# Weight-gradient blocks of a window-attention backward pass over six quads instead of three, one per step in one pair of PSUM banks

## The chip, the cores and the metric

The kernel runs on one core of a Trainium2 chip. The metric is the device time in microseconds (us) of the whole kernel; lower is better. Eight runs of the kernel before have a median of 2055.7 us (2049.22 to 2061.59).

## The reference

A picture of 256 × 256 points with C = 384 channels is cut into 1024 windows of 8 × 8 = 64 points. Each window does single-head attention with one projection for q, k, v and an output projection. The result is the output and, for a given gradient of it, the gradients of x, wqkv and wo.

```python
qkv = xw @ wqkv                                   # xw: 1024 windows x 64 points x 384
q, k, v = (qkv[..., :C].copy(), qkv[..., C:2 * C].copy(), qkv[..., 2 * C:].copy())
p = _softmax(jnp.einsum('bqc,bkc->bqk', q, k) * scale, axis=-1)
o = jnp.einsum('bqk,bkc->bqc', p, v) @ wo
...
_out, _vjp = jax.vjp(_f, x, wqkv, wo)
_grads = _vjp(grad_out)
```

All tensors are bf16.

## The kernel before, in words

**Tiles.** A "quad" is a block of 16 × 32 points, that is 8 windows, held as 4 tiles of 128 rows (two windows each) by 384 channels. There are 128 quads, and the main loop is `step(n)` for n = 0 to 127. Weights are folded once at the start: A = scaled Wq·Wkᵀ (with its transpose AT) and B = Wv·Wo (with BT), so that scores need one projection of x, and the gradient of the scores one projection of the output gradient DO.

**What a step does.** Step n works on three quads at once. For quad n it makes MD (`md`, L188: x and the turned probabilities TT), the two parts V and W that the weight gradients need together with most of dx (`attn`, L220, from P in PB), the rest of dx (`dxs`, L253) and the output (`outs`, L201). For quad n+2 it makes the scores and the softmax (`scores`, `chain0`, `chain2`, `chain3`, L127 to L161). For quad n+3 it projects x and DO (`proj`, L109) into YHT. P of quad n+1 is turned on TensorE (`turn_p`, L163): 16 small transposes into the upper half of PSUM bank 2, which one VectorE copy (L171) takes to TT for the `md` of the next step.

**Weight gradients.** X of a quad and its VW (the V and W parts, 384 columns each) give six products of 128 × 384, numbered k = 0 to 5: three row blocks of X (ma) for V, three for W. `wgrad` (L273) sums one such product over the 12 tiles of a group of three quads, as four matmuls of 64 rows by 64 columns per tile; the two window halves go to two PSUM banks. `wgrad_add` (L265) then adds both banks into ACC in SBUF by two VectorE instructions (L271). A group's six blocks enter the list `todo` when its last quad is done; each step takes two: the first in banks 4 and 7, ahead of the first half of attention (`attn2(n, 0)`), the second in banks 3 and 4, ahead of `turn_p` and of `attn2(n, 1)`. Steps with an empty list (the first three) take another way, called early.

**What sets the order.** The program runs under a manual schedule: every engine does its instructions in the order in which the program issues them, and waits are put in by what they read and overwrite. PSUM has eight banks of 512 fp32 columns. A half of attention uses banks 0 to 2 for V and W (two tiles of 768 columns) and part of banks 5 to 7 for dx (from column 5·512, 384 per tile). Tiles 2 and 3 overwrite banks 0 to 2, so they wait for ScalarE's copies of tiles 0 and 1 (`vw_ev`, L244), and tile 3 in bank 2 waits for the copy of the turned P. `MB` (L186) names the bank pairs of `md`. Banks are evacuated by ScalarE (L80) and VectorE (L82).

**DMA.** SyncE (SP) issues, in this order per step, the load of DO for quad n+5, the transposes of X and DO for n+4 (`turn_in`, into XT and DOT) and, after each projection, the transposes of YHT for n+3 (`turn_yh`, into YH). GpSimd (POOL) issues the load of X for n+5 and the stores of dx (DXS) and of the output (OS), and does the last two operations of P. Everything that crosses steps is a ring, indexed by the quad's number modulo its size: X 11, DO 6, XT 3, DOT 2, YHT 2, YH 3 (NTOK), VW 6.

Of the kernel before, what the change touches and what calls it, by code (L numbers as in the profile page):

```python
# [9 lines left out]
ALU = mybir.AluOpType  # L10
AX = mybir.AxisListType
BF16 = mybir.dt.bfloat16
# [4 lines left out]
def kernel(  # L17
# [12 lines left out]
    _, H, W, C = x.shape  # L30
    P = 128
    CK = C // P
# [2 lines left out]
    NQC = W // 32  # L35
    NQ = (H // 16) * NQC
    scale = float(C) ** -0.5
    GQ = 3
    groups = [tuple(range(q, q + GQ)) for q in range(0, NQ - GQ, GQ)]
    groups += [(q,) for q in range(len(groups) * GQ, NQ)]  # L40
    NX, ND, NXT, NDT, NYH, NTOK, NVW = 11, 6, 3, 2, 2, 3, 6
    PE, DVE, ACT, POOL, SP = nc.tensor, nc.vector, nc.scalar, nc.gpsimd, nc.sync

    sb = ctx.enter_context(tc.tile_pool(name="sb", bufs=1))
# [1 line left out]
    PS = pp.tile([P, 8, 512], F32, name="PS")  # L46
    PSF = PS[:].rearrange("p b c -> p (b c)")
    X = sb.tile([P, NX * 4, C], BF16, name="X")
# [26 lines left out]
    def mm(out, lhsT, rhs, start, stop):  # L75
        PE.matmul(out, lhsT=lhsT, rhs=rhs, start=start, stop=stop, skip_group_check=True)  # L76
# [15 lines left out]
    def load_x(q, n):  # L92
        for t in range(4):
            q.dma_start(out=X[:, (n % NX) * 4 + t, :], in_=img(x, n, t))  # L94

    def load_do(q, n):
        for t in range(4):
            q.dma_start(out=DO[:, (n % ND) * 4 + t, :], in_=img(grad_out, n, t))
# [6 lines left out]
    def turn_yh(n, a):  # L105
        SP.dma_start_transpose(out=YH[:, n % NTOK, a, :, :],
                               in_=YHT[:, n % NYH, a, :, :].rearrange("p m t -> p (m t)"))

    def proj(n, a, banks, engs):  # L109
        wgt = A_sb if a == 0 else BT_sb  # L110
        src = (XT[:, n % NXT] if a == 0 else DOT[:, n % NDT]).rearrange("p (t m) k -> p m t k", m=CK)
        i = 0
        for mo in range(CK):
            for t0, t1 in ((0, 4),) if mo < CK - 1 else ((0, 2), (2, 4)):
                o = PS[:, banks[i], 0:P * (t1 - t0)]
                for m in range(CK):
                    mm(o.rearrange("p (t k) -> p t k", k=P), wgt[:, m, mo * P:(mo + 1) * P], src[:, m, t0:t1, :],
                       m == 0, m == CK - 1)
                ev(engs[i], YHT[:, n % NYH, a, mo, P * t0:P * t1], o)
                i += 1  # L120

    def stack(n, a, m0, m1):

        dst = HYS[:, 4 * m0:4 * m1, 0::3, :] if a == 0 else HYS[:, 4 * m0:4 * m1, 1:3, :]
        DVE.tensor_copy(out=dst, in_=YHT[:, n % NYH, a, m0:m1, :].rearrange("p m (t w k) -> p (m t) w k", w=2, k=64))  # L125
# [16 lines left out]
    def chain0(n):  # L142
        for w in range(2):
            DVE.tensor_reduce(out=ST[HALF[w], 0, :], in_=sd(w, w), axis=AX.X, op=ALU.max)  # L144
        for w in range(2):
            DVE.tensor_tensor(out=SS[HALF[w]], in0=sd(w, w),  # L146
                              in1=ST[HALF[w], 0, :].unsqueeze(2).to_broadcast([64, 4, 64]), op=ALU.subtract)

    def chain2(n):
        ACT.activation(out=PEX[:], in_=SS[:], func=ACTF.Exp)  # L150
# [10 lines left out]
        POOL.tensor_tensor(out=pb[:, 0], in0=TM[:], in1=UM[:], op=ALU.subtract)  # L161

    def turn_p(n):  # L163
        bb = PS[:, 2, 256:512].bitcast(BF16)
        for t in range(4):
            for a in range(2):
                for w in range(2):
                    r = slice(64 * w, 64 * w + 64)
                    o = t * P + a * 64
                    PE.transpose(bb[r, o:o + 64], PB[r, n % 2, a, t, :], ident[r, r])  # L170
        DVE.tensor_copy(out=TT[:, n % 2, :, :, :].rearrange("p t a k -> p (t a k)"), in_=bb)  # L171
# [11 lines left out]
        pturn(XT[:, n % NXT] if a == 0 else DOT[:, n % NDT],  # L183
              lambda j: nat[:, j // CK, (j % CK) * P:(j % CK + 1) * P], banks, engs)

    MB = ((2, 3), (1, 6), (0, 5))  # L186

    def md(n):  # L188
        for m in reversed(range(CK)):
# [57 lines left out]
    def attn2(n, h):  # L247
        for t in (2 * h, 2 * h + 1):
            attn_vw(n, t, t % 2 * 2 * C)
        for t in (2 * h, 2 * h + 1):  # L250
            vw_ev(n, t, t % 2 * 2 * C, ACT)
# [10 lines left out]
            for w in range(2):  # L262
                POOL.dma_start(out=img(out_1, n, t)[8 * w:8 * w + 8], in_=DXS[64 * (1 - w):64 * (1 - w) + 64, n % 2, t, :])  # L263

    def wgrad_add(g, k, banks):  # L265
        for i, b in enumerate(banks):
            if g == 0 and i == 0:
                DVE.tensor_copy(out=ACC[:, k, :], in_=PS[:, b, 0:C])
            else:
                last = g == len(groups) - 1 and i == len(banks) - 1  # L270
                DVE.tensor_tensor(out=GF[:, k, :] if last else ACC[:, k, :], in0=PS[:, b, 0:C], in1=ACC[:, k, :], op=ALU.add)  # L271

    def wgrad(g, k, banks):  # L273

        which, ma = k // CK, k % CK
        tiles = [(q, t) for q in groups[g] for t in range(4)]
        for i, (q, t) in enumerate(tiles):
            s0, s1 = i == 0, i == len(tiles) - 1
            xs, vs = (q % NX) * 4 + t, (q % NVW) * 4 + t
            if len(banks) == 1:  # L280
                mm(PS[:, banks[0], 0:C], X[:, xs, ma * P:(ma + 1) * P], VW[:, vs, which, :], s0, s1)
                continue
            for hh in range(2):
                for w in range(2):
                    r, o = slice(64 * w, 64 * w + 64), slice(64 * hh, 64 * hh + 64)
                    mm(PS[o, banks[w], 0:C], X[r, xs, ma * P + hh * 64:ma * P + hh * 64 + 64], VW[r, vs, which, :], s0, s1)

    todo = []

    def fill(*banks):  # L290

        left = 4 * GQ
        for b in banks:
            if todo and left >= 4 * len(groups[todo[0][0]]):
                g, k = todo.pop(0)
                wgrad(g, k, (b,))
                wgrad_add(g, k, (b,))
                left -= 4 * len(groups[g])

    flat = VW[:].rearrange("p a b c -> p (a b c)")  # L300
    wT = flat[:, 0:JK * C].rearrange("p (j c) -> p j c", j=JK)
# [16 lines left out]
    def step(n):  # L318
        S, A = n + 2, n + 3
        doS, doA = S < NQ, A < NQ  # L320
        early = not todo
        if n + 5 < NQ:
            load_do(SP, n + 5)
            load_x(POOL, n + 5)
        if n + 4 < NQ:
            turn_in(n + 4, 0)
            turn_in(n + 4, 1)

        md(n)
        if early:  # L330
            if doA:
                proj(A, 0, (7, 4, 0, 5), (ACT, ACT, ACT, DVE))
            if n + 1 < NQ:
                turn_p(n + 1)
            attn_vw(n, 0, 0)
            vw_ev(n, 0, 0, ACT)
            attn_vw(n, 1, 2 * 512)
            attn_vw(n, 2, 2 * 512 + 2 * C)
            vw_ev(n, 1, 2 * 512, DVE)
            vw_ev(n, 2, 2 * 512 + 2 * C, ACT)  # L340
            attn_vw(n, 3, 0)
            vw_ev(n, 3, 0, ACT)
            if doA:
                turn_yh(A, 0)
            if doS:
                stack(S, 0, 0, 3)
                stack(S, 1, 0, 3)
        else:
            g, k = todo.pop(0)
            wgrad(g, k, (4, 7))  # L350
            wgrad_add(g, k, (4, 7))
            attn2(n, 0)
            if doS:
                stack(S, 0, 0, 3)
                stack(S, 1, 0, 3)
            g, k = todo.pop(0)
            wgrad(g, k, (3, 4))
            if n + 1 < NQ:
                turn_p(n + 1)
            wgrad_add(g, k, (3, 4))  # L360
            attn2(n, 1)

        dxs(n, 0)
        dxs(n, 1)
        if doS:
            scores(S)
            chain0(S)
        dxs(n, 3)
        dxs_ev(n, 0, ACT)
        dxs(n, 2)  # L370
        if doS:
            chain2(S)
        dxs_ev(n, 1, ACT)
        if doS:
            chain3(S)
        if early and doA:
            proj(A, 1, (0, 1, 2, 4), (ACT, ACT, ACT, DVE))
            turn_yh(A, 1)
        elif doA:
            proj(A, 0, (0, 1, 2, 4), (ACT, ACT, ACT, DVE))  # L380
            turn_yh(A, 0)
        else:
            fill(0, 1, 2)
        outs(n, 0, (5, 6), ACT)
        outs(n, 2, (4, 7) if early else (0, 1), ACT)
        outs_st(n)
        if not early and doA:
            proj(A, 1, (7, 2, 4, 3), (ACT, ACT, ACT, DVE))
            turn_yh(A, 1)
        elif not doA:  # L390
            fill(7, 2, 4)
        g = [g for g in groups if g[-1] == n]
        if g:
            todo.extend((groups.index(g[0]), k) for k in range(2 * CK))

    def gate(ap):
        POOL.tensor_copy(out=ST[0:1, 3, 0:1], in_=ap)
# [1 line left out]
    with tc.manual_schedule():  # L399
# [12 lines left out]
        for n in (1, 2):  # L412
            load_x(POOL, n)
            load_do(POOL, n)
        load_do(SP, 3)
        load_x(POOL, 3)
        load_do(SP, 4)
        load_x(POOL, 4)
        for i in range(12):
            mm(PS[:, 7, :], wsrc[:, 0:P], wsrc, True, True)  # L420

# [42 lines left out]
        chain2(1)  # L464
        chain3(1)
        proj(2, 0, (0, 1, 4, 5), (ACT, ACT, ACT, ACT))
        turn_yh(2, 0)
        proj(2, 1, (6, 7, 0, 4), (ACT, ACT, ACT, ACT))
        turn_yh(2, 1)
        for n in range(NQ):  # L470
            step(n)
            if n == 4:
# [1 line left out]
                    SP.dma_start_transpose(out=woT_sb[:, :, m * P:(m + 1) * P], in_=wo[m * P:(m + 1) * P, :])  # L474


        for b in (3, 4, 5, 6, 7, 3):
            fill(b)

        def ep(o, lt, rr, dst, eng, sc):  # L480
            for mb in range(CK):
# [65 lines left out]
```

## Time and profile before

| | value |
|---|---|
| median of 8 runs | 2055.7 us |
| the profiled execution: its own time | 2061.59 us |
| its span | 2059.8 us |
| TensorE clock granted | 0.999 |
| adds into ACC (L271): count, mean of one | 502, 555 ns |
| DMA queue 1 (SyncE's): share of 16 engines | 80.9% |
| DMA queue 0 (POOL's): share of 16 engines | 27.5% |
| landing after issue: YH, XT, DOT; X, DO | 6.6, 6.0, 5.8 us; 5.4, 5.4 us |

The profile is of one execution. Busy time counts an instruction from its start to its end, for a matmul to its modelled end, so a matmul that stands waiting for its output bank counts as busy. "PE" is matmuls, "PEld" weight loads; "issue" is idle time for which the profile shows no cause. In the timeline a row merges instructions of one kind: start, time covered, engine, line, what it writes and reads, shape, count, and in brackets the idle time before it and what ended it. "SPq" is SyncE's queue of DMA issues. The DMA share can exceed 1, since the packets of two queues overlap on one engine.

### The profile page before, as it was taken

How to read it: one execution, taken by the hardware profiler on the slowest of the kernel's cores; microseconds unless marked ns; L12 is line 12 of the kernel's file. 1: busy time of each engine (PE TensorE's matmuls, PEld its weight loads, DVE VectorE, ACT ScalarE, POOL GpSimd, SP SyncE). 2: the span in 40 equal slices, each digit the busy share in tenths (PEclk: the TensorE clock that was granted, in tenths of full speed). 3: DMA queues.
4: the chain of work that ended last, by engine and by line, in shares of the span. 5: the costliest groups of instructions: out<-in, count | busy, mean ns of one | idle time of the engine just before them, and what ended most of it. 6: DMA issues, size and time to landing. Idle time of an engine off the chain costs nothing.

```text
span 2059.8 us, 90483 instructions
## 1 busy us (share of the span) xinstructions
PE 2012.2 (98%) x38593; PEld 1482.2 (72%) x38593; DVE 1313.9 (64%) x2843; ACT 1360.2 (66%) x2329; POOL 1296.2 (63%) x2315
## 2 busy tenths in 40 slices
PE   8899999999999999999999999999999999999998
PEld 5577777777777777777777777777777777777775
DVE  5566666666666666666666666666666666666664
ACT  5666666666666666666766666666666666666664
POOL 4666666666666656666665666666666666666644
PEclk9999999999999999999999999999999999999999
DMA  9999999999999999999999999999999999999982
GB/s 207 206 197 193 205 197 204 214 193 208 201 206 206 203 202 204 206 207 201 207 203 210 203 203 202 203 208 201 208 204 198 207 208 197 208 205 203 202 150 70
DMA packets 972308, 410.00 MB, mean 199 GB/s; under 512 B 855296, under 2 KB 947264, under 8 KB 971904
## 3 DMA queue, kind: packets, MB, share of 16 engines
q1 hardware_dynamic: 871632, 251.17, 80.9%
q0 software_dynamic: 98496, 151.78, 27.5%
q8 instruction: 301, 4.93, 1.0%
q10 hardware_dynamic: 1776, 1.28, 0.2%
q14 instruction: 103, 0.84, 0.1%
HBM read 101.84 MB, written 101.84 MB: 99 GB/s over the span
## 4 chain that ended last, share of the span: by engine, by line
PE 93%; DVE 4%; issue 1%; ACT 1%; DMA 1%; DVEq 0%; ACTq 0%
PE PS L76 91%; DVE TT L171 3%; PE PS L170 2%; DMA X<-in_x_dram 0%; DVE HYS L125 0%; DMA XT<-X 0%; DVE SS L146 0%; DVE ST L144 0%; DVE TM L158 0%; ACT OS L80 0%; ACT DXS L80 0%; ACT VW L484 0%; DVE VW L82 0%; DVEq L171 0%; DVE YHT L82 0%
## 5 line engine op out<-in xcount | busy, mean ns | idle before, releaser
L263 POOL DMA_DIRECT2D out_dram<-DXS x1024 | 577.9, 571 | 687.3 <-ACT DXS L80 661.1
L80 ACT CAST VW<-PS 128x768 bf16<-128x768 f32 x509 | 381.9, 802 | 373.9 <-PE PS L76 371.4
L76 PEld LDWEIGHTS <-X 64*64 64x64 bf16 x18216 | 532.5, 107 | 105.4 <-issue 59.6
L76 PE MATMUL PS<-VW,X 64*64 64x384 bf16 (+1 forms) x12072 | 585.2, 323 | 2.3 <-issue 2.3
L76 PEld LDWEIGHTS <-MD 128*128 128x128 bf16 x3840 | 335.1, 98 | 177.1 <-issue 35.6
L80 ACT CAST YHT<-PS 128x512 bf16<-128x512 f32 (+1 forms) x770 | 358.9, 523 | 8.0 <-PE PS L76 6.7
L271 DVE TENSOR_TENSOR ACC<-PS,ACC 128x384 f32<-128x384 f32 x502 | 278.8, 555 | 108.3 <-PE PS L76 90.6
L76 PE MATMUL PS<-AT_sb,MD 128*128 128x384 bf16 (+2 forms) x2304 | 296.0, 273 | 2.4 <-issue 1.4
L210 POOL DMA_DIRECT2D out_dram<-OS x512 | 276.0, 546 | 15.4 <-issue 9.2
L94 POOL DMA_DIRECT2D X<-in_x_dram x508 | 272.1, 554 | 14.8 <-issue 11.2
L76 PE MATMUL PS<-B_sb,MD 128*128 128x384 bf16 x1536 | 272.1, 327 | 5.4 <-DVE YHT L82 3.8
L76 PE MATMUL PS<-XT,A_sb 128*128 128x512 bf16 (+1 forms) x1536 | 271.6, 327 | 3.5 <-issue 2.6
L76 PE MATMUL PS<-DOT,BT_sb 128*128 128x512 bf16 (+1 forms) x1536 | 270.5, 326 | 0.0
L82 DVE CAST MD<-PS 128x512 bf16<-128x512 f32 x384 | 241.5, 684 | 11.5 <-PE PS L76 11.5
L82 DVE CAST YHT<-PS 128x256 bf16<-128x256 f32 (+1 forms) x254 | 107.1, 422 | 213.6 <-PE PS L76 210.8
L76 PE MATMUL PS<-YH,PB 64*64 64x128 bf16 (+2 forms) x4084 | 241.1, 246 | 0.2 <-issue 0.2
L76 PEld LDWEIGHTS <-BT_sb 128*128 128x128 bf16 x1536 | 149.9, 98 | 112.5
L76 PE MATMUL PS<-X,PB 64*64 64x256 bf16 (+2 forms) x2036 | 210.6, 245 | 17.6
L80 ACT CAST MD<-PS 128x512 bf16<-128x512 f32 x384 | 200.2, 594 | 33.2 <-PE PS L76 33.2
L76 PEld LDWEIGHTS <-PB 64*64 64x64 bf16 x8168 | 187.7, 107 | 47.4 <-issue 45.8
L76 PEld LDWEIGHTS <-A_sb 128*128 128x128 bf16 x1536 | 144.9, 98 | 102.5 <-issue 4.2
L80 ACT CAST DXS<-PS 128x768 bf16<-128x768 f32 x256 | 202.2, 790 | 20.1 <-PE PS L76 3.1
(65 smaller groups left out, 1889.0 us busy)
## 6 DMA issues: line engine op xcount, KB each, us to landing
out_dram<-DXS POOLq DMA_DIRECT2D x1024, 48.0 KB, 3.3
out_dram<-OS POOLq DMA_DIRECT2D x512, 96.0 KB, 3.7
X<-in_x_dram POOLq DMA_DIRECT2D x508, 96.0 KB, 5.4
DO<-in_grad_out_dram SPq DMA_DIRECT2D x504, 96.0 KB, 5.4
YH<-YHT SPq DMA_TRANSPOSE x256, 6.6
XT<-X SPq DMA_TRANSPOSE x126, 6.0
DOT<-DO SPq DMA_TRANSPOSE x126, 5.8
DO<-in_grad_out_dram POOLq DMA_DIRECT2D x8, 96.0 KB
```

The costliest lines, as they stand in the source:

```text
L76: PE.matmul(out, lhsT=lhsT, rhs=rhs, start=start, stop=stop, skip_group_check=True)
L80: ACT.copy(out=out, in_=in_)
L82: DVE.tensor_copy(out=out, in_=in_)
L94: q.dma_start(out=X[:, (n % NX) * 4 + t, :], in_=img(x, n, t))
L170: PE.transpose(bb[r, o:o + 64], PB[r, n % 2, a, t, :], ident[r, r])
L171: DVE.tensor_copy(out=TT[:, n % 2, :, :, :].rearrange("p t a k -> p (t a k)"), in_=bb)
L210: POOL.dma_start(out=img(out_0, n, t), in_=OS[:, n % 2, t, :])
L263: POOL.dma_start(out=img(out_1, n, t)[8 * w:8 * w + 8], in_=DXS[64 * (1 - w):64 * (1 - w) + 64, n % 2, t, :])
L271: DVE.tensor_tensor(out=GF[:, k, :] if last else ACC[:, k, :], in0=PS[:, b, 0:C], in1=ACC[:, k, :], op=ALU.add)
```

## The change

- Blocks reach over six quads (24 tiles). Each step takes one block, in banks 3 and 4 alone: half of its tiles ahead of `attn2(n, 0)`, the other half after `turn_p` and ahead of `attn2(n, 1)`; the adds come after `attn2(n, 1)`. V groups start at quads 0, 6, ..., W groups at 3, 9, ... (the first W group has three quads), so every third step puts three blocks on the list, now in the middle of the step (`ready`). The last two quads are groups of their own.
- `turn_p` writes bank 7 instead of 2 and comes before the block's second half, right after `attn2(n, 0)`. `MB[0]` is (2, 7) instead of (2, 3); the early projection uses bank 3 instead of 7.
- The load of DO for n+5 goes from the head of the step to after attention, the load of X for n+5 to after the block (ahead of `attn2(n, 1)`). YHT is turned for quad n+2 in one pair after attention, where it was turned for n+3 after each projection.
- In a step that is not early, the exponential (`chain2`) and all of `chain0` come after the second copy of dx; in early steps the scores come after all of `dxs`, and the second projection is copied by ScalarE alone.
- Rings: X 13, DO 5, YH 2, VW 9.

```diff
-    GQ = 3
-    groups = [tuple(range(q, q + GQ)) for q in range(0, NQ - GQ, GQ)]
-    groups += [(q,) for q in range(len(groups) * GQ, NQ)]
-    NX, ND, NXT, NDT, NYH, NTOK, NVW = 11, 6, 3, 2, 2, 3, 6
+    GQ = 6
+    NX, ND, NXT, NDT, NYH, NTOK, NVW = 13, 5, 3, 2, 2, 2, 9
...
+    groups = [cut(0), [tuple(range(GQ // 2))] + cut(GQ // 2)]
...
     def turn_p(n):
-        bb = PS[:, 2, 256:512].bitcast(BF16)
+        bb = PS[:, 7, 256:512].bitcast(BF16)
...
-    MB = ((2, 3), (1, 6), (0, 5))
+    MB = ((2, 7), (1, 6), (0, 5))
...
+    class Block:
+        def __init__(self, which, g, ma):
+            self.k, self.which, self.ma = which * CK + ma, which, ma
+            self.first, self.last = g == 0, g == len(groups[which]) - 1
+            self.tiles = [(q, t) for q in groups[which][g] for t in range(4)]
...
+    def ready(n):
+        for which in range(2):
+            for g, quads in enumerate(groups[which]):
+                if quads[-1] == n:
+                    todo.extend(Block(which, g, ma) for ma in range(CK))
...
     def fill(*banks):
-        left = 4 * GQ
+        left = 12
...
-        if n + 5 < NQ:
-            load_do(SP, n + 5)
-            load_x(POOL, n + 5)
         if n + 4 < NQ:
             turn_in(n + 4, 0)
             turn_in(n + 4, 1)
...
             if doA:
-                proj(A, 0, (7, 4, 0, 5), (ACT, ACT, ACT, DVE))
+                proj(A, 0, (3, 4, 0, 5), (ACT, ACT, ACT, DVE))
...
-            g, k = todo.pop(0)
-            wgrad(g, k, (4, 7))
-            wgrad_add(g, k, (4, 7))
+            blk = todo.pop(0)
+            nb = len(blk.tiles)
+            blk.mms((3, 4), 0, nb // 2)
             attn2(n, 0)
             if doS:
                 stack(S, 0, 0, 3)
                 stack(S, 1, 0, 3)
-            g, k = todo.pop(0)
-            wgrad(g, k, (3, 4))
             if n + 1 < NQ:
                 turn_p(n + 1)
-            wgrad_add(g, k, (3, 4))
+            blk.mms((3, 4), nb // 2, nb)
+            if n + 5 < NQ:
+                load_x(POOL, n + 5)
             attn2(n, 1)
+            blk.add((3, 4))
+        ready(n)
+        if n + 5 < NQ:
+            load_do(SP, n + 5)
+        if doS:
+            turn_yh(S, 0)
+            turn_yh(S, 1)
 
         dxs(n, 0)
         dxs(n, 1)
-        if doS:
+        if doS and not early:
             scores(S)
-            chain0(S)
         dxs(n, 3)
-        dxs_ev(n, 0, ACT)
+        if not early:
+            dxs_ev(n, 0, ACT)
         dxs(n, 2)
-        if doS:
-            chain2(S)
+        if early:
+            dxs_ev(n, 0, ACT)
+            if doS:
+                scores(S)
         dxs_ev(n, 1, ACT)
         if doS:
+            chain0(S)
+            chain2(S)
             chain3(S)
-        if early and doA:
-            proj(A, 1, (0, 1, 2, 4), (ACT, ACT, ACT, DVE))
-            turn_yh(A, 1)
-        elif doA:
-            proj(A, 0, (0, 1, 2, 4), (ACT, ACT, ACT, DVE))
-            turn_yh(A, 0)
+        if doA:
+            proj(A, int(early), (0, 1, 2, 4), (ACT, ACT, ACT, ACT if early else DVE))
```

## The prediction

> **What bounds the kernel now.** I read the page first, for who is busy and what the last chain is made of:
>
> ```profile
> PE 2012.2 (98%) x38593; PEld 1482.2 (72%) x38593; DVE 1313.9 (64%) x2843; ACT 1360.2 (66%) x2329; POOL 1296.2 (63%) x2315
> DMA  9999999999999999999999999999999999999982
> PE PS L76 91%; DVE TT L171 3%; PE PS L170 2%; DMA X<-in_x_dram 0%; DVE HYS L125 0%; DMA XT<-X 0%; DVE SS L146 0%; DVE ST L144 0%; DVE TM L158 0%; ACT OS L80 0%; ACT DXS L80 0%; ACT VW L484 0%; DVE VW L82 0%; DVEq L171 0%; DVE YHT L82 0%
> ```
>
> TensorE sets the end, but a fixed 3% of the chain runs through VectorE's copy of the turned P (TT, L171), and the DMA engines are as full as TensorE. The chain in order of time, over one step, shows where that copy lies:
>
> ```profile
> 1019.90 0.29 PE PS L170 x12
> ...
> 1020.39 0.44 DVE TT L171
> 1020.86 14.64 PE PS L76 x260
> 1035.50 0.29 PE PS L170 x12
> ```
>
> From one turn of P to the next it is 35.50 − 19.90 = 15.60 us, and 128 such steps are 1997 us of the 2059.8 us span. 14.64 us of it is matmul; the rest is turn, copy, release. The timeline of that place (start, us, engine) shows what TensorE loses:
>
> ```profile
> 1017.28 1.22 DVE L271 TENSOR_TENSOR ACC<-PS,ACC 128x384 f32<-128x384 f32 x2 [0.64 <-PE PS L76]
> ...
> 1017.62 2.41 PE L76 MATMUL PS<-VW,X 64*64 64x384 bf16 x48
> ...
> 1017.89 1.76 PEld L76 LDWEIGHTS <-X 64*64 64x64 bf16 x46 [0.25 <-issue]
> ...
> 1019.71 0.47 PE L170 MATMUL PS<-ident,PB 64*64 64x64 bf16 x13
> ...
> 1020.39 0.42 DVE L171 COPY TT<-PS 128x512 bf16<-128x512 bf16 x1 [0.90 <-PE PS L170]
> ...
> 1020.46 0.65 PE L76 MATMUL PS<-X,PB 64*64 64x256 bf16 x3
> ...
> 1021.21 1.16 PE L76 MATMUL PS<-AT_sb,MD 128*128 128x384 bf16 x9
> ```
>
> Two waits show. The second gradient block starts at 1017.62, but its second bank (4) is still being added by the L271 pair, so its weights stand still for 0.25 us until 1017.89, just after the first add ended. And the second half of attention hangs at 1020.46: a matmul that alone takes 0.27 us covers 0.65, because its output shares bank 2 with the P that L171 is copying out until 1020.81. The first half of attention, the same work, began at 1016.96 and took 1017.62 − 1016.96 = 0.66 us; the second took 1021.21 − 1020.02 = 1.19.
>
> **The change, part by part.** *Block and turn.* Now: block 2, turn, attention half 2 take 1021.21 − 1017.62 = 3.59 us. After: attention half 1, turn, second half of the one block, attention half 2. The block half opens no bank anew, so it costs what the unhindered block costs: 1016.96 − 1015.01 = 1.95 us. The turn costs 0.31 (1019.71 to 1020.02; by its 16 matmuls between 0.2 and 0.4 in its new place, I take 0.31). Attention half 2 costs 0.66 plus the gap ahead of the 128-row matmuls that follow (0.255 after its last matmul, against 0.057 between 64-row pieces), so 0.86. Sum 3.12; gain 0.47 us a step. The copy of TT (0.42) is now covered by the 1.95 us half block; without that cover the old 0.4 us stall would be back. VectorE is free for it: its MD copies end some 0.8 us ahead of the turn, and both first-block adds, 1.22 us, are gone from between. What is late next there: the VW copies on ScalarE, which end at 1017.65 + 1.50 = 1019.15, while half 2 would start near 1019.9. No wait.
>
> *Rows of MB.* The third MD group goes to bank 7 in place of 3, whose YHT copy VectorE ends only at 1014.76, into md. In the single records of the trace md's first matmul on bank 3 comes 0.113 us after its predecessor, where 0.03 to 0.05 is usual: gain 0.08 (0 if the copy of bank 7 were late; it is ScalarE's first of four, a microsecond earlier). The block's first bank is then 3, at 1014.93, still after that copy. The early steps' first projection swaps 7 for 3: no effect.
>
> *Adds.* Twice the quads per block halve the adds: about 240 of 502, at 555 ns, some 133 us off VectorE. They lay beside matmul work, apart from the bank-4 wait counted above: nothing more. The two adds now stand after attention half 2; scores (bank 3) come 0.86 + 0.99 us after the block ends, and the first add takes 0.56: covered by dxs.
>
> *Softmax.* The exponential goes behind the second DXS copy on ScalarE, 0.79 us. ScalarE idles 1.8 us ahead of it now, for SS, and dxs of tile 2 is done by then: 0, and at worst 0.8, which the 3.2 us between the end of PB on GpSimd (1014.44) and the turn's new place (1017.62) cover.
>
> *Loads and turns by DMA.* The X load moves behind the block on GpSimd; only every third step does its ring of 13 make it wait for that block. Behind it are the DXS stores and P's last two operations. GpSimd idles 4.86 us ahead of the DXS stores and the load takes 2.13: 0. On SyncE the DO load (4.1 us) now waits for attention half 2, about 6.4 us into the step; behind it stand both YH turns, then XT and DOT of the next step. The YH turns land 6.6 us after issue, so about 16 to 18 us into step n; the first needs to be done before YHT is rewritten 25 us in, and YH is read 33 us in. So SyncE may fall some 9 us behind before TensorE notices. Cost 0 while the DMA engines keep pace; that is the open point.
>
> *Ends.* Steps 3 to 5 get half blocks (3 × 1.95 = 5.9 us less), and steps 125 to 127 get that back. Early steps (their copies of TT lie 14.7 us apart) no longer pass the softmax between projections, about 4 us of chain each of which matmuls can fill maybe 2. Between −7 and +6; I take 0, since the DMA is full there.
>
> **Is there room in the DMA queue?** The SyncE queue early in the run:
>
> ```profile
> 169.46 2.75 SPq L98 DMA_DIRECT2D DO<-in_grad_out_dram  x4
> 172.44 4.05 SPq L102 DMA_TRANSPOSE XT<-X  x1
> 176.59 2.09 SPq L102 DMA_TRANSPOSE DOT<-DO  x1
> 178.78 6.32 SPq L106 DMA_TRANSPOSE YH<-YHT  x2
> 185.15 3.12 SPq L98 DMA_DIRECT2D DO<-in_grad_out_dram  x4
> ```
>
> Here it issues without a pause and one round takes 15.69 us; twelve rounds, 124.9 to 313.2, average 15.69 at a DMA share of 1.21. Around 1002 to 1190 the share is 1.11, and the queue, by its own records of waits, pauses about 2.5 us a step. Counting packets in flight, the engines then lack work for some 0.8 us a step. So the DMA's own period lies between about 14.8 and 15.7 us, and the new TensorE step, 15.60 − 0.47 − 0.08 = 15.05, lies inside. The Trainium skill (DMA: Bandwidth & Descriptors, Latency and other measured facts) gives DMA transposes 261 GB/s: 393 KB takes an estimated 1.5 us, the four of a step 6.0. By that SyncE would idle half the step, and I would give the 15.05 almost for certain. The rows have SyncE at the four for 9 to 12 us, so they decide, and the DMA stays a rival. In that full stretch TensorE also shows gaps under "issue" (1.04 us at 216.31, 1.36 at 317.89), each just after a packet of the instruction queue; the skill (Runtime: NRT & Kernel Launch, Instruction fetch mechanics) calls that fetch mostly hidden. Five or six of them cost about 5 us in those twelve steps, against three in the hundred steps after. With less DMA slack I allow 4 us in all (0 to 40).
>
> **Sum.** 123 steps × 0.55 = 68 us. Ends 0, longer fetches +4. The profiled execution, 2061.6 us, would become 2061.6 − 64 = 1997.6; from the median 2055.7 it is 1991.7. I say 1992.
>
> **Rivals.**
> *DMA takes part of it (0.24).* SyncE's turns now run in one piece beside the stores, as in the early stretch. With a DMA period of 15.35 a step, TensorE waits for it: gain 0.25 × 123 = 31, about 2025. For: the share of 1.21. Against: after a late step (800.7) a round took only 14.27.
> *DMA makes it slower (0.15).* The held-back DO load leaves SyncE idle in the one stretch in which no store is in flight, and the round stays at the bad early length. If rounds are 15.75 us, TensorE waits at the YHT rewrite each step: +0.15 × 123 = 18, about 2074. It decides from a round above 15.60.
> *The stall moves (0.07).* If something else, the copies of VW or the open banks, holds attention half 2 as long as TT did, only the bank waits go: within some 4 us of 2055. Against: the 0.75 us of room above.
>
> **How the numbers follow.** 0.54 for the sum as it stands: from 1976 (ends at −7, the turn 0.07 us shorter: −9) to 2012 (ends at +6, 14 us more of fetch gaps). The range runs from there over the DMA case to 2058, and leaves out the slower rival and a little below: 1976 to 2058. Faster by over 0.2% (about what a measurement of this kernel tells from no change): 0.54 + 0.24 = 0.78; same 0.07; slower 0.15.
>
> **What would show it.** Right: the chain has no TT, the step from turn to turn is 15.0 to 15.1 us, the weights of the block stand still nowhere, attention half 2 takes about 0.86 to dxs. Wrong: matmuls of the projections or copies of YHT that wait for DMA YH or XT, SyncE's queue without pauses, a step of 15.3 or more, many "issue" gaps; or half 2 of attention still longer than half 1, with VW named.

## The result, and the profile after

The kernel after takes 2036.8 us (median of 11 runs, 2026.43 to 2048.07) against 2055.1 us before (median of 32): 0.991 times, 95% interval 0.990 to 0.993. The direction held and the time lies in the range, but the gain is 18 us where 63 were forecast. In the profiled executions the span went from 2059.8 to 2036.1 us. (That of before was the slowest of its runs, so 23.7 us here answer to 18 between medians.)

The page of the kernel after, its lines on engines, the instruction queue (packets, MB, share), the chain by engine and by line, and the adds among the costliest groups:

```profile
PE 1956.6 (96%) x38449; PEld 1431.6 (70%) x38449; DVE 1184.4 (58%) x2592; ACT 1378.9 (68%) x2332; POOL 1307.2 (64%) x2315
...
q8 instruction: 300, 4.92, 1.0%
...
PE 93%; issue 3%; ACT 1%; DMA 1%; DVE 1%; ACTq 0%; DVEq 0%
PE PS L86 91%; PE PS L180 1%; DMA YH<-YHT 1%; ACT YHT L90 0%; ACT VW L90 0%; DVE MD L92 0%; DMA X<-in_x_dram 0%; ACT DXS L90 0%; DVE SS L156 0%; DVE ST L154 0%; ACT VW L509 0%; ACT MD L90 0%; ACT OS L90 0%; DVE HYS L135 0%; ACTq L104 0%
...
L304 DVE TENSOR_TENSOR ACC<-PS,ACC 128x384 f32<-128x384 f32 x254 | 141.7, 558 | 232.1 <-PE PS L86 218.8
```

TT's 3% is gone from the chain, as forecast, and the adds are 254, where about 240 were. But TensorE's share of busy time fell from 98 to 96%, and 3% of the chain is now "issue". The chain in order of time, in one good step of the kernel after:

```profile
1407.23 0.18 PE PS L180 x11
...
1407.48 14.64 PE PS L86 x279
1422.12 0.18 PE PS L180 x11
```

From turn to turn it is 1422.12 − 1407.23 = 14.89 us: less than the 15.05 forecast. So far the argument held. The timeline of that place:

```profile
1403.75 0.86 PE L86 MATMUL PS<-TT,X 64*64 64x128 bf16 x48
1404.45 2.12 PE L86 MATMUL PS<-VW,X 64*64 64x384 bf16 x48
...
1407.06 0.35 PE L180 MATMUL PS<-ident,PB 64*64 64x64 bf16 x11
...
1407.31 2.12 PE L86 MATMUL PS<-VW,X 64*64 64x384 bf16 x46
```

The md (from TT), the first half block, attention, the turn and the second half block follow each other without a hole: the second half block starts 0.25 us after the turn (L180) began. In another step the same chain reads:

```profile
1018.50 2.29 PE PS L86 x62
1020.78 1.33 issue
1022.11 12.60 PE PS L86 x220
...
1035.77 1.22 issue
```

In about every other step, around the turn and the block's halves, TensorE stands still for about a microsecond and nothing that the profile knows released it. In the timeline of the first of these two places it is in the middle of attention half 2, between two groups of matmuls that read the same P and YH as those just before them:

```profile
1020.44 0.34 PE L86 MATMUL PS<-DO,PB 64*64 64x128 bf16 x6
1022.11 0.24 PE L86 MATMUL PS<-YH,PB 64*64 64x128 bf16 x2 [1.33 <-issue]
```

How often: what TensorE's queue waited for, 110 to 1980 us (us in total, times, longest). Before:

```profile
PE PS L76 <- issue: 5.3, 9, 1.4
```

After:

```profile
PE PS L86 <- issue: 54.0, 56, 3.4
```

**Which wait this is.** I counted the matmuls and weight loads of each trace in order of time. Over the same stretch the kernel after has 60 gaps of over 0.45 us between two starts; 58 of them end at an instruction whose number leaves 191 when divided by 256. All 8 of before do, too. TensorE's 2 × 38,449 = 76,898 instructions make 300.4 blocks of 256, and the instruction queue (q8) carries 300 packets, each of 16,384 bytes. In the step above the packet started at 1019.69 and took 1.09 us; TensorE went on at 1022.11. Over the 60 gaps it goes on 1.2 to 2.1 us after a packet's end, 1.44 in the middle, and nowhere in this trace does it pass such a place sooner than 1.18 us after it. So TensorE has run through a block of its program before the next block is there.

**The account.** Of the steps 6 to 121 of after, 38 take 14.89 us to the hundredth, and the mean is 15.58 (before: most 15.60 or 15.61, mean 15.69). In 115 steps: 0.71 us less in the good step is −82 us; the gaps grew from 0.05 to 0.57 us a step, +60; waits of under 0.45 us, about +10, of which two short stretches of a lower granted clock (0.62 from 349.5 to 354 us, 0.66 from 400.5 to 405.5) are some 3.4. The mean falls by 0.105 us, 12.1 us in all. The five steps from the turn in step 0 to that in step 5 give another 12.6 us (14.1 us a step instead of 16.6), what lies before them 2.5, and what lies behind the 115 steps takes back 3.5. Sum: −23.7, the change of the span.

### The profile page after: what moved, and what is told of

It is laid out like the page before. It is cut to its first block, busy times and chain, and to the rows that moved or that the text cites. A ratio compares the mean times of both kernels' runs of the same rounds, so it can differ in the third digit from the quotient of the medians.

```text
span 2036.1 us, 90420 instructions
## 1 busy us (share of the span) xinstructions
PE 1956.6 (96%) x38449; PEld 1431.6 (70%) x38449; DVE 1184.4 (58%) x2592; ACT 1378.9 (68%) x2332; POOL 1307.2 (64%) x2315
## 3 DMA queue, kind: packets, MB, share of 16 engines
q1 hardware_dynamic: 871632, 251.17, 81.9%
## 4 chain that ended last, share of the span: by engine, by line
PE 93%; issue 3%; ACT 1%; DMA 1%; DVE 1%; ACTq 0%; DVEq 0%
PE PS L86 91%; PE PS L180 1%; DMA YH<-YHT 1%; ACT YHT L90 0%; ACT VW L90 0%; DVE MD L92 0%; DMA X<-in_x_dram 0%; ACT DXS L90 0%; DVE SS L156 0%; DVE ST L154 0%; ACT VW L509 0%; ACT MD L90 0%; ACT OS L90 0%; DVE HYS L135 0%; ACTq L104 0%
## 5 line engine op out<-in xcount | busy, mean ns | idle before, releaser
L86 PE MATMUL PS<-VW,X 64*64 64x384 bf16 x11928 | 563.9, 323 | 20.2 <-issue 19.8
L86 PEld LDWEIGHTS <-X 64*64 64x64 bf16 x18072 | 481.0, 107 | 129.1 <-issue 51.5
L104 POOL DMA_DIRECT2D X<-in_x_dram x508 | 280.9, 565 | 31.1 <-DMA out_dram<-DXS 12.1
L90 ACT CAST DXS<-PS 128x768 bf16<-128x768 f32 x256 | 206.4, 807 | 124.9 <-PE PS L86 114.9
L304 DVE TENSOR_TENSOR ACC<-PS,ACC 128x384 f32<-128x384 f32 x254 | 141.7, 558 | 232.1 <-PE PS L86 218.8
L90 ACT CAST OS<-PS 128x768 bf16<-128x768 f32 x256 | 204.3, 799 | 79.7 <-PE PS L86 76.5
L86 PE MATMUL PS<-YH,PB 64*64 64x128 bf16 (+2 forms) x4084 | 217.8, 243 | 7.1 <-issue 7.1
L154 DVE TENSOR_REDUCE ST<-PS 64x4 f32<-64x256 f32 x256 | 107.9, 422 | 188.9 <-PE PS L86 179.4
```

Of the source, the lines that this page charges most:

```text
L90: ACT.copy(out=out, in_=in_)
L304: DVE.tensor_tensor(out=GF[:, self.k, :] if last else ACC[:, self.k, :], in0=PS[:, b, 0:C], in1=ACC[:, self.k, :], op=ALU.add)
```

## The experiments

Three theories stood against each other:
- **A:** TensorE waits for its own instructions, since the dense stretch (md, half block, attention, turn, half block, attention) runs through 256 instructions faster than the next block comes through full DMA engines.
- **B:** the DMA engines themselves take about 15.5 us a round, so nothing done on TensorE can make the step shorter.
- **C:** the new order on SyncE's queue, not the denser TensorE, makes instructions late.

The ratio is to the kernel before, on the same chip. "Good step" is from turn to turn without a gap. "Gaps" is what gaps of over 0.45 us between two TensorE starts cost beyond the usual spacing, per step.

| kernel | time, us | ratio [95% interval] | good step | mean step | gaps, us a step |
|---|---|---|---|---|---|
| before | 2055.1 | 1 | 15.60 | 15.69 | 0.05 |
| after | 2036.8 | 0.991 [0.990, 0.993] | 14.89 | 15.58 | 0.57 |
| e1, before, turn alone | 2042.8 | 0.995 [0.993, 0.996] | 15.51 | 15.57 | 0.47 |
| e2, after, turn put back | 2046.2 | 0.996 [0.994, 0.998] | 15.22 | 15.56 | 0.29 |
| e3, after, hardly any output stores | 2040.1 | 0.993 [0.990, 0.996] | 14.89 | 15.57 | 0.60 |
| e5, after, blocks in 64 × 128 | 2012.1 | 0.979 [0.978, 0.981] | 15.34 | 15.37 | 0.04 |
| e6, after, other order on SyncE | 2042.4 | 0.993 [0.990, 0.995] | 14.89 | 15.56 | 0.54 |
| e7, after, md and blocks in 64 × 128 | 2003.1 | 0.974 [0.971, 0.977] | 15.22 | 15.21 | 0.02 |
| e8, after, md and half of each block | 2008.8 | 0.977 [0.973, 0.980] | 14.99 | 15.30 | 0.29 |
| e9, before, blocks in 64 × 128 | 2073.8 | 1.009 [1.006, 1.011] | 15.82 | 15.82 | 0.00 |
| e10, e8 and e6 together | 1985.2 | 0.967 [0.964, 0.969] | 14.99 | 15.10 | 0.09 |
| e11, after, no turns of YHT | 1967.4 | 0.958 [0.956, 0.960] | 14.89 | 14.96 | 0.05 |
| e12, e7 and e6 together | 2002.0 | 0.975 [0.973, 0.976] | 15.22 | 15.24 | 0.03 |

### e1: the turn of P alone

In the kernel before, P is turned in bank 7 right after the first half of attention; both three-quad blocks use banks 3 and 4.

```diff
-        bb = PS[:, 2, 256:512].bitcast(BF16)
+        bb = PS[:, 7, 256:512].bitcast(BF16)
...
-            wgrad(g, k, (4, 7))
-            wgrad_add(g, k, (4, 7))
+            wgrad(g, k, (3, 4))
+            wgrad_add(g, k, (3, 4))
...
-            g, k = todo.pop(0)
-            wgrad(g, k, (3, 4))
             if n + 1 < NQ:
                 turn_p(n + 1)
+            g, k = todo.pop(0)
+            wgrad(g, k, (3, 4))
```

> The kernel before with the turn alone: P is turned into bank 7 right after the first half of attention, MB[0] is (2, 7), both gradient blocks of three quads use banks 3 and 4. Rings, loads and DMA order stay as before. The unhindered step should be about 15.2 us (15.60 less the copy's stall and the md wait, plus some 0.3 for bank 4, which is still being added). Theory A (TensorE's instruction fetch: with the stall gone TensorE runs through its dense stretch faster than a full DMA brings the next block of instructions): gaps of about 1 us at block boundaries come up here too, 0.2 to 0.6 us a step, 2025 to 2050 us. Theory C (the new order of SyncE's queue delays the fetch): few gaps, as before, about 2005 to 2015 us.

It came to 2042.8 us. The chain of this kernel in order of time shows a new stall in the old one's place:

```profile
1001.41 0.57 DVE ACC L271
...
1002.03 14.84 PE PS L76 x277
...
1016.93 0.57 DVE ACC L271
```

Every step now waits for the add of the first block, since the second one reopens the same banks: 15.51 us a step, nearly the old 15.60, and that wait is the 0.47 us a step in the table. Only 5 gaps lie at block boundaries of the program. The time lies in the range that was given for A, but not for A's reason, so the run doesn't tell A from C: the new wait keeps TensorE as slow as TT did. What it does show is why one long block per step, opened once, is needed for the turn's early place to bring anything.

### e2: the turn put back

In the kernel after, the turn is again in bank 2, behind the whole block.

```diff
-        bb = PS[:, 7, 256:512].bitcast(BF16)
+        bb = PS[:, 2, 256:512].bitcast(BF16)
...
+            blk.mms((3, 4), nb // 2, nb)
             if n + 1 < NQ:
                 turn_p(n + 1)
-            blk.mms((3, 4), nb // 2, nb)
```

> The changed kernel with the turn of P back in bank 2 and behind the block's second half: the stall of attention behind the copy returns, about 0.4 us, so the unhindered step goes from 14.89 to about 15.3 us. Theory A: the stall lies in the dense stretch and gives the fetch its time, so gaps fall and the time stays within 15 us of the changed kernel, about 2025 to 2050 us. Theory C: gaps stay at 0.57 us a step and the stall adds 0.4 x 123 = 50, about 2085 us. Theory B (DMA data bound, a round of 15.5 us whatever TensorE does): 2037 us.

The good step grew by 0.33 us, to 15.22, but the time by only 9 us, where 0.33 × 123 = 41 would be its price. The mean step is 15.56, that of after. What the stall costs, the gaps give back: 0.29 us a step instead of 0.57. In the waits of this kernel, over the same stretch:

```profile
PE PS L86 <- issue: 23.6, 37, 2.0
```

It is A's sign: the wait for TT, while it lasted, was time in which instructions arrived. It isn't the whole of it: with the stall back the gaps are still 0.29 us a step, where the kernel before had 0.05.

### e3: without the stores of the output

In the kernel after, the output of only the first and the last quad is stored: 360.4 MB move instead of 410.0.

```diff
-        for t in range(4):
+        for t in range(4 if n in (0, NQ - 1) else 0):
```

> The changed kernel, but the stores of out_0 (OS, four a step of 96 KB) are left out for all quads but the first and the last; the output picture stays unwritten. Theories A and B: with a third of POOL's bytes gone the engines have room, gaps nearly vanish, steps go to 14.9 to 15.0 us, about 1960 to 1975 us. If gaps come from TensorE's stream alone and not from the DMA: gaps stay, about 2035 us.

The stores' absence brings nothing: 2040.1 us, 63 gaps.

```profile
PE PS L86 <- issue: 55.7, 57, 2.6
```

The stretch from 200 to 1900 us (start and end, length, busy us and count of PE, PEld, DVE, ACT, POOL; clock, DMA share, GB/s), after:

```profile
200.00:1900.00 1700.00, 1642.98 (x32921) 1209.43 (x32912) 993.91 (x2180) 1163.01 (x1963) 1110.93 (x1962) 1.00 1.17 206
```

and without the stores:

```profile
200.00:1900.00 1700.00, 1643.74 (x32947) 1212.12 (x32945) 994.21 (x2187) 1165.82 (x1970) 875.90 (x1534) 1.00 1.08 180
```

The share fell from 1.17 to 1.08 and 26 GB/s less moved, and TensorE did the same work in that stretch (32,947 matmuls against 32,921). What was expected here of A failed: this much less traffic does not bring the blocks of instructions in time. It does bring some of them sooner, but not those that are short of time: counted as under "Arrival against need" below, blocks that TensorE enters 5 to 7.5 us into a step, where it takes over 9 us for one, come after 4.69 us instead of 5.86; those it enters with md come after 4.50 instead of 4.28.

### e5: blocks in 64 × 128

In the kernel after, a tile of a block is two matmuls of 64 rows by 128 columns, not four of 64 by 64. The products are the same.

```diff
-                for hh in range(2):
-                    for w in range(2):
-                        r, o = slice(64 * w, 64 * w + 64), slice(64 * hh, 64 * hh + 64)
-                        mm(PS[o, banks[w], 0:C], X[r, xs, self.ma * P + hh * 64:self.ma * P + hh * 64 + 64],
-                           VW[r, vs, self.which, :], s0, s1)
+                for w in range(2):
+                    r = slice(64 * w, 64 * w + 64)
+                    mm(PS[:, banks[w], 0:C], X[r, xs, self.ma * P:(self.ma + 1) * P],
+                       VW[r, vs, self.which, :], s0, s1)
```

> The changed kernel with the gradient block as two matmuls of 64 rows by 128 columns per tile instead of four of 64 by 64: the same sums in the same banks, 96 fewer TensorE instructions per step (of some 600), all in the dense stretch. Theory A: fewer fetches and more time for each, gaps fall from 0.57 to under 0.25 us a step, about 1990 to 2005 us if the other tile shape costs nothing[...]. Theory B: no gain from it, 2037 us or later.

Its chain in order of time, from turn to turn:

```profile
1001.73 0.24 PE PS L180 x16
1001.97 15.10 PE PS L86 x238
1017.07 0.24 PE PS L180 x16
```

A step of 15.34 us, held in nearly every step (mean 15.37), with no "issue" left among the waits of TensorE's matmuls from 110 to 1980 us, at a DMA share of 1.17 as in after. The good step is 0.45 us longer: a half block of 24 matmuls takes 2.05 us to the next matmul where 48 take 1.95, and the other changes of shape cost about 0.1 us each. Yet the kernel is 25 us faster than after: a slower TensorE program of 96 instructions less a step. The gaps fell as A expected; the time is 7 us above its range of 1990 to 2005, which took the shape to be free. B falls: the DMA engines keep a round of 15.34. It also counts fewer packets, 254 in q8 for 2 × 32,545 / 256 = 254.3 blocks.

### e6: another order on SyncE

In the kernel after, the load of DO goes back to the head of the step, a quad later, and all transposes (YHT, then X and DO) stand after attention.

```diff
-        if n + 4 < NQ:
-            turn_in(n + 4, 0)
-            turn_in(n + 4, 1)
+        if n + 4 < NQ and n:
+            load_do(SP, n + 4)
...
-        if n + 5 < NQ:
-            load_do(SP, n + 5)
         if doS:
             turn_yh(S, 0)
             turn_yh(S, 1)
+        if n + 4 < NQ:
+            turn_in(n + 4, 0)
+            turn_in(n + 4, 1)
```

> The changed kernel with SyncE's queue in another order: the load of DO (for n+4) at the head of the step, all four transposes (YH twice, XT, DOT) behind attention, so that the loads and not the XT and DOT turns fall into TensorE's dense stretch. Theory C (what is in flight in the dense stretch delays the fetch, and the order put transposes there): gaps fall below 0.2 us a step, about 1990 us. Theory A in its narrow form (256 instructions run through in 4.1 us where 4.5 are needed, whatever is in flight): gaps stay at 0.4 to 0.6 us a step, 2025 to 2045 us.

The same stretch of this kernel:

```profile
200.00:1900.00 1700.00, 1650.27 (x32992) 1214.74 (x32990) 997.52 (x2191) 1168.81 (x1973) 1112.90 (x1972) 1.00 1.08 206
```

```profile
PE PS L86 <- issue: 52.4, 64, 2.8
```

The share fell from 1.17 to 1.08 and the gaps stay: 0.54 us a step, 2042.4 us. So this order does not cure them, and C fails in the form tested here. The order of the kernel before, under after's program for TensorE, was not run; the table on arrival below shows why C isn't quite out.

### e7, e8 and e9: how many instructions, and where

e7 adds the 64 × 128 form in md to e5. e8 has it in md and in the first half of the block alone, so that no shape changes between the second half, the turn and attention. e9 is the control: the kernel before with e5's edit.

```diff
-                for hh in range(2):
-                    for w in range(2):
-                        r = slice(64 * w, 64 * w + 64)
-                        mm(PS[64 * hh:64 * hh + 64, MB[m][w], t * P:t * P + P],
-                           X[r, (n % NX) * 4 + t, m * P + hh * 64:m * P + hh * 64 + 64],
-                           TT[r, n % 2, t, :, :], True, True)
+                for w in range(2):
+                    r = slice(64 * w, 64 * w + 64)
+                    mm(PS[:, MB[m][w], t * P:t * P + P], X[r, (n % NX) * 4 + t, m * P:(m + 1) * P],
+                       TT[r, n % 2, t, :, :], True, True)
```

> The changed kernel with both the block and md as matmuls of 64 rows by 128 columns: 144 fewer TensorE instructions a step, and no change of shape between md and the block. Theory A: next to no gaps, and the step of 15.34 us (block alone in that shape) loses the 0.1 us between md and block and some of md: 15.1 to 15.2 us, about 1982 to 1992 us. If the gain of the block's shape had nothing to do with the number of instructions, gaps may come back.

> The changed kernel with md and the first half of the block as 64 rows by 128 columns, the second half as before: 96 fewer TensorE instructions a step, at the head of the dense stretch, for one more change of shape. Theory A: few gaps (under 0.15 us a step) and a step of 15.0 to 15.1 us, about 1972 to 1985 us. If what counts is the second half of the stretch, from the turn on, where the instructions stay as dense: gaps of 0.3 us or more, 2005 us or later.

> A control: the kernel before with both its blocks as 64 rows by 128 columns, 96 fewer instructions. Theory A: before has hardly any fetch gaps to lose (0.05 us a step), so only the changes of shape count, 0.3 to 0.45 us a step: slower, 2085 to 2110 us. If the shape is faster by itself: under 2055 us.

e7: 2003.1 us, 15.22 us in nearly every step and next to no gaps, but slower than the 1982 to 1992 expected. e8: 2008.8 us, with a good step of 14.99 as expected, but with gaps of 0.29 us a step instead of under 0.15, and so far above the 1972 to 1985 of A. Of its 35 gaps 19 are at no block boundary. The page's line on its chain names them:

```profile
PE PS L86 83%; DMA YH<-YHT 9%; PE PS L180 1%; DMA XT<-X 1%; ACT YHT L90 1%; DVE MD L92 0%; DMA DOT<-DO 0%; DMA w_sb<-in_wqkv_dram 0%; ACT VW L90 0%; POOL X L104 0%; POOL DO L108 0%; ACT DXS L90 0%; DMA out_dram<-OS 0%; ACT VW L513 0%; DVE SS L156 0%
```

Here TensorE has become fast enough for the rival of the prediction, the late turns of YHT. e9: 2073.8 us, 0.9% slower than before. The kernel before had hardly any gaps to lose, so 64 × 128 costs there what its shapes cost (15.82 us a step instead of 15.60), though less than the 2085 to 2110 us that A had put it at. So it is the new density, not the form, that makes 64 × 128 pay.

### e10, e11 and e12: both cures, and fewer transposes

e10 is e8 with e6's order, e12 is e7 with it. e11 is the kernel after without the turns of YHT from the third quad on; dx then comes out of the YH of the first two quads, and only the time counts.

```diff
-        if doS:
-            turn_yh(S, 0)
-            turn_yh(S, 1)
```

> The kernel with md and half of the block as 64 rows by 128 columns, and SyncE's queue with the DO load at the head of the step and all four transposes behind attention. Its step without gaps was 14.99 us, and late YH and XT turns showed in its chain. If these late turns came of the queue's order: they vanish, gaps stay at 0.2 to 0.3 us a step, 1985 to 2000 us. If the DMA engines simply can't keep a step of 15.0 us: within 8 us of 2009.

> The changed kernel, but YH is turned for the first two quads alone; all later quads read those (dx and the weight gradients come out of wrong data). Half of the transposes' packets are gone. If what is in flight sets how late the instruction blocks arrive: the start of a fetch comes earlier, gaps fall below 0.2 us a step, about 1975 to 1995 us. If a fetch takes its 4 to 4.5 us whatever the DMA load, as without the output stores: gaps stay at 0.5 us or more, 2025 to 2040 us.

> The kernel with md and the whole block as 64 rows by 128 columns (its step was 15.22 us, held in nearly all steps), and the DO load at the head of the step, all four transposes behind attention. There is nothing left for the order to gain in the steps, only at the start: 1995 to 2008 us, beside 2003.

e10 is the best of all kernels here that compute everything: 1985.2 us, 3.3% less than before. On its page TensorE is back at 99%, and its chain by line has no YH:

```profile
PE 1955.2 (99%) x32425; PEld 1397.6 (70%) x32425; DVE 1179.5 (59%) x2592; ACT 1379.6 (70%) x2332; POOL 1304.6 (66%) x2315
```

and the chain in order of time stays near 14.99 us a step (1021.74 − 1006.64 = 15.10 here):

```profile
1006.64 0.18 PE PS L180 x12
...
1006.88 14.85 PE PS L86 x228
1021.74 0.18 PE PS L180 x12
```

The waits for YH are gone, and the gaps fell further than the 0.2 to 0.3 us a step that were expected to stay, to 0.09. The order that was of no use alone (e6) is worth its place once the gaps are filled. e12 gains nothing over e7, whose 15.22 us step was TensorE's own.

e11 has after's TensorE program to the instruction, and the good step of 14.89 is now the usual one (mean 14.96); at 1967.4 us it came out below its range of 1975 to 1995. Its page on DMA, queue 1 and the waits of its TensorE:

```profile
DMA  9788878777788778788787887877777777877832
...
q1 hardware_dynamic: 476496, 152.04, 46.5%
```

```profile
PE PS L86 <- issue: 5.4, 11, 1.0
```

With 395,136 of queue 1's 871,632 packets gone, the 56 waits for instructions of after are 11. e3 took away stores, without effect on the time; e11 takes away two of a step's four transposes, and the gaps go. So two transposes a step less are enough to bring the blocks in time. That a block stands behind the transposes' packets themselves is not shown: e11 also takes away much more of the DMA's load (share 0.78) than e3 did (1.08).

**Arrival against need.** For each block of 256 that TensorE enters within the first microsecond of md, I took from the traces how long TensorE runs through it if nothing is late, and when the next is there (end of the packet + 1.45 us), counted from entry; both are means. The gaps (over 0.3 us) are those at the end of these blocks, in after nearly half of all:

| kernel | blocks | run through in, us | next one there after, us | gaps |
|---|---|---|---|---|
| before | 50 | 4.23 | 3.84 | 3 |
| after | 53 | 3.70 | 4.28 | 30 |
| e1 | 52 | 4.07 | 3.69 | 3 |
| e2 | 54 | 3.99 | 4.18 | 23 |
| e3 | 54 | 3.67 | 4.50 | 38 |
| e6 | 53 | 3.68 | 4.53 | 39 |
| e8 | 28 | 5.00 | 3.53 | 0 |
| e10 | 28 | 5.01 | 3.79 | 0 |
| e11 | 54 | 3.63 | 3.18 | 2 |

Wherever the first time exceeds the second, there are at most 3 gaps; wherever it is below, 23 to 39. The change took 0.53 us from the one, about the waits that it removed, and the other rose by 0.44. The two ways to mend it are in the table: fewer instructions for the work (e8, e10), or fewer transposes (e11).

Two things in the traces speak against too simple a reading. e1 and e2 have the same mean step (15.57 and 15.56), but e1, with before's order of DMA issues, has the next block at 3.69 us and e2, with after's, at 4.18: the new order may have its part in the 0.44. And inside the trace of after, blocks did not come later when more transposes were in flight: of the 283 blocks that TensorE enters between 110 and 1980 us, the quarter with the fewest transposes in the 3 us after entry had its packet's end after 3.75 us, the quarter with the most after 2.90; the first had the more of GpSimd's stores and loads beside it (a share of 0.52 against 0.17). Both go with the place in the step, so neither is shown to be the cause.

## Why the prediction was right and wrong

**Block and turn: right, and more than forecast.** 3.12 us were forecast for turn, half block and half 2 of attention; 2.97 were measured (before 3.59). The turn adds only 0.19 us of its own, not 0.31, since the block's first matmuls overlap it. Nothing was late next there: the copies of VW appear with 0% in the chain.

**Rows of MB: right.** md went from 0.79 to 0.69 us, 0.10 where 0.08 was forecast. Both together, with what small overlaps bring: 0.71 us a good step where 0.55 was forecast.

**Adds, softmax, loads on GpSimd: right at nothing.** They are in no wait of the steady steps.

**Ends: outside the bounds, in part perhaps by luck.** 0 was taken, −7 at best; outside the 115 steps the profiled execution gained 11.6 us. The early steps, "about 4 us of chain each of which matmuls can fill maybe 2", gained only 0.6 each (14.71 to 14.07). Steps 3 to 5, put at 5.9 for their half blocks, gained 11.4: before's profiled execution lost 3.0 us there in two "issue" gaps (1.03 and 2.01), and some 1.7 to a lower granted clock (0.91 from 88.16 to 107.60 us). These 4.7 us need not be the change's.

**The fetch: the step that failed.** "With less DMA slack I allow 4 us in all (0 to 40)" is the term. It measured +60 us. The rows it drew on were there: the gaps of 1.0 and 1.4 us just after packets of the instruction queue, in the full stretch. I took their number to follow from how full the DMA engines are alone, and so scaled 3 gaps in a hundred steps by a little. But a gap needs both: when the next block comes, and how fast TensorE gets through the one it has. Before, TensorE took 4.23 us for such a block and the next was there after 3.84. The margin was 0.4 us, the stall that was to be removed took as much, and it lay in this very stretch. Counting the instructions from md to attention half 2 against the packets would have shown the margin gone; that the packets would also come 0.44 us later could not be seen there. The Trainium skill (Runtime: NRT & Kernel Launch, Instruction fetch mechanics), weighed in the prediction, calls fetch mostly hidden; the trace of before agreed (0.05 us a step), that of after does not (0.57).

**The rivals.** The time, 2037, lies between that of the case "DMA takes part of it" (2025) and "the stall moves" (2055), but neither happened. The chain runs through a turn of YHT (DMA YH) in two places alone, at 260.12 and 277.23 us. e5 holds a step of 15.34 with after's order of transfers and hardly a wait (0.04 us a step), and e10 one of 15.10 with all the transfers in e6's order: the DMA engines' own period is no longer than these. SyncE's pauses did shrink, from 2.6 to 1.9 us a step, as that case expected. The stall did move, though not to a copy or a bank: to the arrival of TensorE's instructions. "Many 'issue' gaps" was among the signs of being wrong, and is the one that came.

**What stays open.** That TensorE waits for its instructions, and that fewer of them or half of the transposes end the wait, is shown; why the blocks come as late as they do is not. Leaving out the turns of YHT brings them in time, leaving out stores or e6's order doesn't. Which packets a block stands behind, and on which of the 16 engines, was not measured. It isn't explained why the next block arrives at 4.28 us in after and 3.84 in before with the same transposes a step, nor why e6, at a share of 1.08, has it at 4.53. e11 also takes away SyncE's issues with the packets, so the two aren't separated. Most of the 0.12 us a step of small waits in after were not apportioned.

## What to carry to other kernels

When a stall is to be taken out of a stretch of many small matmuls, count that stretch's instructions: here TensorE got through a block of 256 in 3.7 us and the next took 4.3 to come, so more than half of what the stall gave back was lost in new waits. A gap that the profile calls "issue", with inputs and banks ready, at the same place modulo 256 and just after a packet of the instruction queue, is this wait; the cure is fewer instructions for the same work, even at a slightly longer good step (e7), or, here, half of the transposes left out (e11). An order of DMA issues that brings nothing alone (e6: ratio 0.993, after 0.991) can be worth 1% once the wait ahead of it is gone (e10 against e8).

## What the hardware showed that was not expected

- TensorE's program came in 300 packets of 16 KB for 76,898 instructions, one for 256; late ones cost about 65 us of 2036, and TensorE went on 1.2 to 2.1 us after the end of a packet, never sooner.
- Taking away nearly all output stores (a DMA share of 1.08 instead of 1.17) did nothing for the packets that TensorE was short of (4.50 against 4.28 us, 63 gaps); taking away half of the transposes (share 0.78) brought them 1.1 us sooner (3.18 against 4.28 us).
- Shape changes cost TensorE little but not nothing: 0.25 us passed from the start of a 64 × 128 half block's last matmul to the 64 × 64 one behind it, where after has 0.08 to 0.15, so that the half block took 2.05 us to that point and not 1.95; e5's good step was 0.45 us longer by two such blocks.
